# A decode block with its gradients: the middle regrouped, and second-pass transposes as products with the identity

## The chip, the cores and the metric

The kernel runs on one core of a Trainium2 chip. The metric is the device time of one execution in microseconds (us). TensorE is called PE here, VectorE DVE, ScalarE ACT, GpSimd POOL and SyncE SP, as in the profile; PEld is PE's loading of weights.

## The reference

One transformer block for a single token per sequence, forward and backward: a layer norm, attention against a cache of 4096 keys and values (batch 2, 32 heads, head size 128), a residual, a second layer norm and an MLP with relu (640 to 1728 to 640). Results are the output and the gradients of seven inputs.

```python
def _fwd_reference(A_x, A_k_cache, A_v_cache, A_wq, A_wo, B_x, B_w1, B_w2):
    ...
        q = (lambda x, *d: x.transpose(*d))((x @ wq).reshape(B, Sq, Hq, Dh), 0, 2, 1, 3)
        scores = jnp.einsum("bhqd,bhkd->bhqk", q, k) * (Dh ** -0.5)
        p = _softmax(scores, axis=-1)
        o = jnp.einsum("bhqk,bhkd->bhqd", p, v)
        return (lambda x, *d: x.transpose(*d))(o, 0, 2, 1, 3).reshape(B, Sq, Hq * Dh) @ wo
    ...
        h = jnp.einsum("bsd,df->bsf", x, w1)
        h = jnp.maximum(h, zero)
        return jnp.einsum("bsf,fd->bsd", h, w2)
    x = A_x
    h = x + _A_ref(_layernorm(x, axis=-1), A_k_cache, A_v_cache, A_wq, A_wo)
    h2 = h + _B_ref(_layernorm(h, axis=-1), B_w1, B_w2)
    return h2

def reference(A_x, A_k_cache, A_v_cache, A_wq, A_wo, B_w1, B_w2, B_x, grad_out):
    ...
    _out, _vjp = jax.vjp(_f, A_x, A_k_cache, A_v_cache, A_wq, A_wo, B_w1, B_w2)
    _grads = _vjp(grad_out)
```

Everything is bf16. The two caches are 64 tiles of 1 MB each (one per batch and head); their gradients, as large, are outer products of a column of length 4096 and a row of length 128.

## The kernel before

A pair is one batch and one head; there are 64. The **first pass** (`p1_iter`, one iteration per pair in a software pipeline three deep) loads a K and a V tile. It transposes K in four groups of eight 128x128 blocks on PE (`transpose_group`, line 264; ACT evicts a group from PSUM at line 269, or DVE at line 267 for the last group of the first iterations), multiplies by q (line 275), takes the softmax, and forms with V the attention output and a 128x128 matrix MT that the backward pass needs (lines 294 and 310, scaled by ACT at line 396). The **second pass** (`p2_iter`, one iteration per pair, index j) loads V again as W, transposes it in the same way, multiplies it by the gradient of the attention output, and forms the gradients gV and gK as outer products on DVE (line 533, two halves each), which POOL's queue stores (lines 577 and 593).

Between the passes stands the **middle** of each batch (`middle_gen`): the product with wo, layer norm, w1, relu, w2, the output row, then backward: the products of grad_out with w2 (`ga`), of the masked result with w1 (`gx2`), the backward layer norm, and products with wo in four groups of eight heads, each of which ends with the mark `("go", b, g)`. Those backward products are done on DVE by `ttr` (line 426), a multiplication with a row that is spread over the partitions (`bcast_cols`), summed along the row. After both middles `fin_gen` forms the weight gradients: `rows_of` (line 611) turns columns to rows, `outer_rows` forms output tiles of up to 512 columns with PE (line 635), evicts them by ACT or DVE (lines 638 and 640) and stores them (line 643); at last five columns of wq are loaded again (line 667), transposed and multiplied (line 676).

The order of all instructions is written out by hand: the generators are run against each other, each engine takes its instructions in that order, and SP issues the loads in the order of a list (`queue`), as tiles come free. The middles and `fin_gen` are background generators in a list `bg`, taken one after the other. After each step of a pass, `bg_step` adds a rate to a credit and runs background steps until the credit is used; a step costs 0.35, or what it yields (0.9 for a `ttr`). A first-pass iteration has 8 such steps, a second-pass one 5. `bg_until` runs the background at once where a pair needs a mark that isn't there. `plan` starts the second pass at first-pass iteration `P2_AT`, in every second iteration, until the first pass ends; from there it runs alone.

PSUM has two buffers for transposes (tag `tps`), three for scores and one each for `m`, `tiny` and `mid`; the background shares `mid`. SBUF has seven tiles of 1 MB for loads and three for gV and gK.

Of the kernel before, what the change touches and what calls it, by code (L numbers as in the profile page):

```python
# [9 lines left out]
ALU = mybir.AluOpType  # L10
# [5 lines left out]
def kernel(  # L16
# [97 lines left out]
    OU = cols.tile([128, B, H, 2], FP32)  # L114
    P_bf = cols.tile([128, B * H, NSC], BF16)
    nc.vector.memset(acol[:], 0.0)
    nc.vector.memset(ghfc[:], 0.0)
# [14 lines left out]
    def ln_fwd(xs, nb, xh, rstd):  # L132

        def st(name, dt=FP32):
            return small.tile([128, nb], dt, tag=f"ln_{name}{nb}", bufs=1, name=f"ln_{name}")
        ssum = st("ssum")
        nc.vector.reduce_sum(out=ssum[:], in_=xs, axis=AX.X)
        t1 = colsum(ssum[:], nb)
        yield
        mean = st("mean")  # L140
        nc.vector.tensor_scalar(out=mean[:], in0=t1[:, 0:nb], scalar1=1.0 / D, scalar2=None, op0=ALU.mult)
        cent = small.tile([128, nb, ND], FP32, tag=f"ln_cent{nb}", bufs=1, name="ln_cent")
        nc.vector.tensor_tensor(out=cent[:], in0=xs, in1=bc(mean[:], ND), op=ALU.subtract)
# [3 lines left out]
        nc.vector.reduce_sum(out=vs[:], in_=sq[:], axis=AX.X)  # L147
        t2 = colsum(vs[:], nb)
# [23 lines left out]
        yield  # L172

    def ln_bwd(gh, xh, rstd, add, dst, nb):

        def t3(name):
# [5 lines left out]
        nc.vector.reduce_sum(out=mm[:, 0, :], in_=gh, axis=AX.X)  # L182
        nc.vector.reduce_sum(out=mm[:, 1, :], in_=prod[:], axis=AX.X)
        t = colsum(mm[:].rearrange("p a b -> p (a b)"), 2 * nb)
        yield
# [8 lines left out]
        nc.vector.tensor_tensor(out=dst.rearrange("p c b -> p b c"), in0=u1[:],  # L194
                                in1=add.rearrange("p c b -> p b c"), op=ALU.add)
        yield

# [62 lines left out]

    def transpose_group(nat, g, dve=False):
        t_ps = pst([128, GT, 128], BF16, "tps", "t_ps")
        for j in range(GT):
            nc.tensor.transpose(t_ps[:, j, :], nat[:, g * GT + j, :], ident_bf[:])  # L264
        t_sb = mats.tile([128, GT, 128], BF16, tag="XT", bufs=5, name="t_sb")
        if dve:
            nc.vector.tensor_copy(out=t_sb[:], in_=t_ps[:])  # L267
        else:
            nc.scalar.copy(out=t_sb[:], in_=t_ps[:])  # L269
        return t_sb  # L270
# [161 lines left out]
    def middle_gen(b):  # L432
# [3 lines left out]
        for c in range(ND):  # L436
            for h in range(H):
                nc.tensor.matmul(a_ps[:, c:c + 1], lhsT=wo_t[:, h, c * 128:(c + 1) * 128], rhs=OFc[:, h, b:b + 1],
                                 start=(h == 0), stop=(h == H - 1))
                if h % 16 == 15:  # L440
                    yield
# [8 lines left out]
        for cf in range(NF):  # L450
            kc = f_kc(cf)
            for c in range(ND):
                nc.tensor.matmul(hf_ps[0:kc, cf:cf + 1], lhsT=w1_t[:, c, cf * 128:cf * 128 + kc],
                                 rhs=x2c[:, c, b:b + 1], start=(c == 0), stop=(c == ND - 1))
            if cf % 4 == 3:
                yield
        nc.vector.tensor_scalar(out=acol[:, 0:NFF, b], in0=hf_ps[:, 0:NFF], scalar1=0.0, scalar2=None, op0=ALU.max)
        if F_rem:
            nc.vector.tensor_scalar(out=acol[0:F_rem, NFF, b:b + 1], in0=hf_ps[0:F_rem, NFF:NF],
                                    scalar1=0.0, scalar2=None, op0=ALU.max)  # L460
        yield
        m_ps = pst([128, ND], FP32, "mid", "mlp_ps")
        for c in range(ND):
            for cf in range(NF):
                kc = f_kc(cf)
                nc.tensor.matmul(m_ps[:, c:c + 1], lhsT=w2_t[0:kc, cf, c * 128:(c + 1) * 128],
                                 rhs=acol[0:kc, cf, b:b + 1], start=(cf == 0), stop=(cf == NF - 1))
            if c % 2 == 1:
                yield
        ml_bf = small.tile([128, ND], BF16, tag="ml_bf", bufs=1, name="ml_bf")  # L470
        nc.vector.tensor_copy(out=ml_bf[:], in_=m_ps[:])
        y_bf = small.tile([128, ND], BF16, tag="y_bf", bufs=1, name="y_bf")
        nc.vector.tensor_tensor(out=y_bf[:], in0=h1c[:, :, b], in1=ml_bf[:], op=ALU.add)
        yield
        store_row(y_bf[:], ND, out_0[b].rearrange("s (c p) -> (s c) p", p=128))
        yield
# [11 lines left out]
        nc.vector.tensor_tensor(out=ghfc[:, :, b], in0=ga[:], in1=mask[:], op=ALU.mult)  # L488
        yield
# [14 lines left out]
        for g in range(H // GH):  # L504
# [7 lines left out]
            nc.vector.tensor_tensor(out=pr[:], in0=goc[:, hs, b], in1=OU[:, b, hs, 0], op=ALU.mult)  # L512
            yield
            d_ps = pst([128, 2, GH], FP32, "mid", "d_ps")
            nc.tensor.matmul(d_ps[:, 0, :], lhsT=ones_f32[:], rhs=pr[:], start=True, stop=True)
# [8 lines left out]
            nc.vector.tensor_scalar(out=GQc[:, hs, b], in0=ud[:], scalar1=SCALE, scalar2=None, op0=ALU.mult)  # L524
            yield ("go", b, g)


# [23 lines left out]

    def p2_iter(j):

        c = S2[j] if j < NP1 else None
        p = S2[j - 1] if j - 1 in S2 else None
        if c is not None:
            b, h = pairs[j]
            go = goc[:, h, b:b + 1]
            if "rb" not in c:
                p2_rows(j)  # L560
            c["T0"] = transpose_group(c["W"], 0)
            gV = take("g", [128, NSC, 128], "gV")
# [9 lines left out]
        if c is not None:  # L572
            c["dp"] = pst([128, NSC], FP32, "sps", "dp_ps")
            c["T1"] = transpose_group(c["W"], 1)
            matvec_group(c["dp"], c.pop("T0"), 0, go)
# [4 lines left out]
        if c is not None:  # L580
            c["T2"] = transpose_group(c["W"], 2)
            matvec_group(c["dp"], c.pop("T1"), 1, go)
# [4 lines left out]
        if c is not None:  # L587
            c["T3"] = transpose_group(c["W"], 3)
            give(c["Wg"])
# [29 lines left out]
    def outer_rows(pool, L, nrow, R, N, out_ap, cc):  # L619
# [4 lines left out]
        for c0 in range(0, cc, grp):  # L624
# [4 lines left out]
            for k in range(gn):  # L629
                n0 = 0  # L630
                while n0 < N:
# [9 lines left out]
                    n0 += nn  # L641
                    yield
            nc.gpsimd.dma_start(out=out_v[:, c0:c0 + gn, :], in_=ot[0:P, 0:gn, :])
# [71 lines left out]

    M0_ITERS = 17
    P2_AT = H + 2 + M0_ITERS
    plan = []
    i = j = 0
# [10 lines left out]
    for n, (ii, jj) in enumerate(plan):  # L730
# [34 lines left out]
    for n, (i, j) in enumerate(plan):  # L765
# [64 lines left out]
```

## Time and profile before

| | |
|---|---|
| Median of 3 runs | 1136.31 us (1134.83 to 1139.74) |
| Profiled execution | 1132.04 us |
| Its span, first to last instruction | 1130.1 us |
| Busy: PE, DVE, ACT, POOL | 75%, 64%, 56%, 9% |
| Read and written | 221.48 MB and 149.13 MB |
| Mean granted PE clock | 0.723 |

Times are those of one profiled execution. A row of the groups gives line, engine, operation and tiles, then the count, the busy time, the mean duration in ns, and the idle time before it with what ended it. The granted clock is the share of full speed that the chip gave PE. A DMA share is the mean busy share of the core's 16 DMA engines.

### The profile page before, as it was taken

To read this page: it belongs to the slowest core of one execution; us is meant where nothing else is said; L and a number is where in the kernel's file an instruction comes from. 1 tells how busy PE (TensorE), PEld (TensorE's weight loads), DVE (VectorE), ACT (ScalarE), POOL (GpSimd) and SP (SyncE) were. 2 spreads that over 40 slices of the span, in tenths; PEclk is the share of its full clock that TensorE was granted. 3 is DMA by queue.
4 is the path that set the end of the run, shared out by engine and by line. 5 is a ranking of instruction groups with operands and counts; after the bars stand their busy time and mean duration, and the time that the engine had idled before them with its cause. 6 is when DMAs were issued, how large, how long until landed. Compare 5 with 4: busy or idle time off the path is not lost.

```text
span 1130.1 us, 32280 instructions
## 1 busy us (share of the span) xinstructions
PE 845.2 (75%) x14111; PEld 724.3 (64%) x14111; DVE 717.7 (64%) x1693; ACT 634.0 (56%) x945; POOL 100.6 (9%) x218
## 2 busy tenths in 40 slices
PE   6999999989889878878673545478887875565572
PEld 5988889988878778778563534354564444454562
DVE  3666666655778778556668789945455452345676
ACT  4565555655756667665373644366666643354562
POOL 0000000000000001001111111111111110001121
PEclk9999998986979898888575766555555555575555
DMA  9999999975777598999999989858897687479987
GB/s 360 370 405 406 408 403 400 392 266 188 273 251 239 218 351 336 351 371 378 364 395 371 385 342 348 327 224 321 312 333 298 268 340 267 178 276 416 388 346 325
DMA packets 59757, 372.70 MB, mean 330 GB/s; under 512 B 5760, under 2 KB 15424, under 8 KB 17376
## 3 DMA queue, kind: packets, MB, share of 16 engines
q1 hardware_dynamic: 38960, 221.50, 52.4%
q0 software_dynamic: 20656, 149.14, 32.5%
q8 instruction: 110, 1.80, 0.6%
q14 instruction: 31, 0.25, 0.1%
HBM read 221.48 MB, written 149.13 MB: 328 GB/s over the span
## 4 chain that ended last, share of the span: by engine, by line
PE 43%; DMA 18%; DVE 17%; issue 10%; ACT 10%; POOL 1%; SPq 0%; ACTq 0%; POOLq 0%; DVEq 0%
PE t_ps L264 17%; PE m_ps L294 9%; DMA out_dram<-gV 9%; DVE gK L533 5%; ACT t_sb L269 5%; DMA Wt<-in_A_v_cache_dram 4%; PE m_ps L310 4%; PE o_ps L635 3%; PE s_ps L275 3%; DVE pk L300 3%; DVE junk L426 3%; DVE gV L533 3%; DMA wqs<-in_A_wq_dram 2%; ACT ot L638 1%; PE rw_ps L611 1%
## 5 line engine op out<-in xcount | busy, mean ns | idle before, releaser
L269 ACT COPY t_sb<-t_ps 128x1024 bf16<-128x1024 bf16 x489 | 488.8, 1015 | 234.4 <-PE t_ps L264 228.4
L264 PE MATMUL t_ps<-ident_bf,Wt 128*128 128x128 bf16 x2048 | 234.0, 285 | 12.6 <-DMA Wt<-in_A_v_cache_dram 12.2
L275 PEld LDWEIGHTS <-t_sb 128*128 128x128 bf16 x4096 | 168.9, 103 | 95.8 <-ACT t_sb L269 89.8
L264 PEld LDWEIGHTS <-Wt 128*128 128x128 bf16 x2048 | 182.0, 130 | 58.6 <-issue 45.3
L300 DVE TENSOR_TENSOR pk<-Kt,ep 128x1024 bf16<-128x1024 bf16 x256 | 174.6, 684 | 39.7 <-ACT ep L343 39.6
L294 PE MATMUL m_ps<-pk,Vt 128*128 128x129 bf16 x2048 | 190.7, 233 | 0.9 <-issue 0.9
L533 DVE TENSOR_TENSOR gV<-rb,pp 128x2048 bf16<-128x2048 bf16 x128 | 156.0, 1218 | 51.7 <-POOL pp L549 18.0
L264 PE MATMUL t_ps<-ident_bf,Kt 128*128 128x128 bf16 x2048 | 173.2, 233 | 7.0 <-DMA Kt<-in_A_k_cache_dram 5.0
L533 DVE TENSOR_TENSOR gK<-rb,gsp 128x2048 bf16<-128x2048 bf16 x128 | 153.2, 1218 | 32.7 <-DMA out_dram<-gV 32.5
L275 PE MATMUL dp_ps<-goc,t_sb 128*128 128x1 bf16 x2048 | 96.9, 168 | 69.0 <-ACT t_sb L269 65.9
L294 PEld LDWEIGHTS <-Vt 128*128 128x128 bf16 x2048 | 134.5, 103 | 6.0 <-issue 1.3
L264 PEld LDWEIGHTS <-Kt 128*128 128x128 bf16 x2048 | 131.8, 104 | 8.9 <-DMA Kt<-in_A_k_cache_dram 5.6
L267 DVE COPY t_sb<-t_ps 128x1024 bf16<-128x1024 bf16 x43 | 29.7, 692 | 110.8 <-PE t_ps L264 105.4
L577 POOL DMA_DIRECT2D out_dram<-gV x64 | 34.2, 535 | 729.4 <-DVE gV L533 694.7
L275 PE MATMUL s_ps<-qc,t_sb 128*128 128x1 bf16 x2048 | 89.4, 164 | 1.4 <-DVE gsp L568 0.4
L396 ACT ACTIVATE MT<-m_ps,rtot 128x128 bf16<-128x128 f32 x64 | 23.5, 368 | 106.3 <-PE m_ps L294 106.3
L640 DVE CAST ot<-o_ps 128x128 bf16<-128x128 f32 (+2 forms) x80 | 33.6, 420 | 71.9 <-PE o_ps L635 70.4
L310 PEld LDWEIGHTS <-Kt 128*128 128x128 bf16 x2048 | 64.5, 97 | 18.7 <-issue 17.4
L310 PE MATMUL m_ps<-ep,Kt 128*128 128x1 bf16 x2048 | 70.9, 164 | 7.0 <-ACT OU L397 6.5
L547 ACT CAST rb<-rb_ps 128x256 bf16<-128x256 f32 x64 | 24.0, 376 | 81.2 <-DVE gK L533 63.9
L638 ACT CAST ot<-o_ps 128x512 bf16<-128x512 f32 (+1 forms) x80 | 47.0, 587 | 22.6 <-PE o_ps L635 20.8
L593 POOL DMA_DIRECT2D out_dram<-gK x64 | 34.1, 532 | 223.5 <-DVE gK L533 210.2
(168 smaller groups left out, 738.0 us busy)
## 6 DMA issues: line engine op xcount, KB each, us to landing
Kt<-in_A_k_cache_dram SPq DMA_DIRECT2D x64, 1024.0 KB, 8.5
Vt<-in_A_v_cache_dram SPq DMA_DIRECT2D x64, 1024.0 KB, 8.4
Wt<-in_A_v_cache_dram SPq DMA_DIRECT2D x64, 1024.0 KB, 8.8
out_dram<-gV POOLq DMA_DIRECT2D x64, 1024.0 KB, 6.4
out_dram<-gK POOLq DMA_DIRECT2D x64, 1024.0 KB, 7.7
wo_t<-in_A_wo_dram SPq DMA_DIRECT2D x4, 1280.0 KB, 11.7
out_dram<-ot POOLq DMA_DIRECT2D x5, 1024.0 KB, 8.9
wqs<-in_A_wq_dram SPq DMA_DIRECT2D x5, 1024.0 KB, 8.1
```

The costliest lines, as they stand in the source:

```text
L264: nc.tensor.transpose(t_ps[:, j, :], nat[:, g * GT + j, :], ident_bf[:])
L269: nc.scalar.copy(out=t_sb[:], in_=t_ps[:])
L275: nc.tensor.matmul(dst[:, sc:sc + 1], lhsT=t_sb[:, j, :], rhs=vec, start=True, stop=True)
L294: nc.tensor.matmul(r["m"][:, 0:129], lhsT=r["V"][:, sc, :], rhs=r["pk"][sc // GT][:, sc % GT, 0:129], start=False, stop=(sc == NSC - 1))
L300: nc.vector.tensor_tensor(out=pk[:, :, 0:128].rearrange("p s (a two) -> p s a two", two=2), in0=p["K"][:, sl, :].rearrange("p s (a two) -> ...
L310: nc.tensor.matmul(r["m"][:, 129:130], lhsT=r["K"][:, sc, :], rhs=r["ep"][:, sc, 0:1], start=(sc == 0), stop=False)
L426: nc.vector.tensor_tensor_reduce(out=junk[0:kc, 0:width], in0=in0, in1=in1, scale=1.0, scalar=0.0, op0=ALU.mult, op1=ALU.add, accum_out=acc)
L533: nc.vector.tensor_tensor(out=pairs_view(dst[:, sl, :]), in0=row.rearrange("p (a two) -> p a two", two=2)[:, None, :, :].to_broadcast([128 ...
L577: nc.gpsimd.dma_start(out=natural(out_3, b, h), in_=gV[:])
L593: nc.gpsimd.dma_start(out=natural(out_2, bp, hp), in_=gK[:])
L635: nc.tensor.matmul(o_ps[0:P, 0:nn], lhsT=L[:, bass.ds(c0 + k, P, step=cc)], rhs=R[:, n0:n0 + nn], start=True, stop=True)
L638: nc.scalar.copy(out=ot[0:P, k, n0:n0 + nn], in_=o_ps[0:P, 0:nn])
```

## The change

- The products of grad_out with w2, which don't depend on the forward pass, leave the middle: a generator `ga_gen` computes them for both batches, as a background of the first pass from iteration 14 on. w2 is loaded first of the weights, then w1, then wo.
- In the middle, the forward product with w2 and the output row come last, behind the four groups of wo. Several places get a second yield between a DVE result and the PE instruction that uses it, and the wo and w1 products yield twice as often.
- `M0_ITERS` goes from 17 to 11, so the second pass starts six first-pass iterations earlier. The rates are new, and a tile of `outer_rows` costs 0.5 of credit, not 0.35. `fin_gen` starts when the second middle has ended.
- Where no first pass runs beside it, the second pass transposes V by plain products with the identity, whose result is float32 in PSUM: four blocks to a PSUM buffer instead of eight, and two evictions for a group.

```diff
+    ga = cols.tile([128, B, NF], FP32)
+    nc.vector.memset(ga[:], 0.0)
...
         nc.vector.reduce_sum(out=ssum[:], in_=xs, axis=AX.X)
+        yield
+        yield
         t1 = colsum(ssum[:], nb)
...
-    def transpose_group(nat, g, dve=False):
-        t_ps = pst([128, GT, 128], BF16, "tps", "t_ps")
-        for j in range(GT):
-            nc.tensor.transpose(t_ps[:, j, :], nat[:, g * GT + j, :], ident_bf[:])
+    def transpose_group(nat, g, dve=False, plain=False):
+
         t_sb = mats.tile([128, GT, 128], BF16, tag="XT", bufs=5, name="t_sb")
-        if dve:
-            nc.vector.tensor_copy(out=t_sb[:], in_=t_ps[:])
-        else:
-            nc.scalar.copy(out=t_sb[:], in_=t_ps[:])
+        n = GT // 2 if plain else GT
+        for k in range(0, GT, n):
+            t_ps = pst([128, n, 128], FP32 if plain else BF16, "tps", "t_ps")
+            for j in range(n):
+                if plain:
+                    nc.tensor.matmul(t_ps[:, j, :], lhsT=nat[:, g * GT + k + j, :], rhs=ident_bf[:],
+                                     start=True, stop=True)
+                else:
+                    nc.tensor.transpose(t_ps[:, j, :], nat[:, g * GT + k + j, :], ident_bf[:])
+            if dve:
+                nc.vector.tensor_copy(out=t_sb[:, k:k + n, :], in_=t_ps[:])
+            else:
+                nc.scalar.copy(out=t_sb[:, k:k + n, :], in_=t_ps[:])
...
-                if h % 16 == 15:
+                if h % 8 == 7:
                     yield
...
-            if cf % 4 == 3:
+            if cf % 2 == 1:
                 yield
...
-        yield
-        m_ps = pst([128, ND], FP32, "mid", "mlp_ps")
...
-        store_row(y_bf[:], ND, out_0[b].rearrange("s (c p) -> (s c) p", p=128))
-        yield
-        gbc = cols.tile([128, D], BF16, tag="rowbc", name="gbc")
-        yield from bcast_cols(one(gc, b), ND, lambda c: 128, gbc)
-        ga = small.tile([128, NF], FP32, tag="ga", bufs=1, name="ga")
-        if F_rem:
-            nc.gpsimd.memset(ga[:], 0.0)
-        for c in range(NF):
-            kc = f_kc(c)
-            ttr(w2_t[0:kc, c, :], gbc[0:kc, :], ga[0:kc, c:c + 1], D, kc)
-            yield 0.9
...
-        nc.vector.tensor_tensor(out=ghfc[:, :, b], in0=ga[:], in1=mask[:], op=ALU.mult)
+        nc.vector.tensor_tensor(out=ghfc[:, :, b], in0=ga[:, b, :], in1=mask[:], op=ALU.mult)
...
             yield ("go", b, g)
+        m_ps = pst([128, ND], FP32, "mid", "mlp_ps")
...
+        store_row(y_bf[:], ND, out_0[b].rearrange("s (c p) -> (s c) p", p=128))
+        yield ("y", b)
+
+    def ga_gen():
+
+        for b in range(B):
+            gbc = cols.tile([128, D], BF16, tag="rowbc", name="gbc")
+            yield from bcast_cols(one(gc, b), ND, lambda c: 128, gbc)
+            for c in range(NF):
+                kc = f_kc(c)
+                ttr(w2_t[0:kc, c, :], gbc[0:kc, :], ga[0:kc, b, c:c + 1], D, kc)
+                yield 0.9
...
-                    yield
+                    yield 0.5
...
-    M0_ITERS = 17
+    M0_ITERS = 11
     P2_AT = H + 2 + M0_ITERS
+    RATES = (0.2, 0.5, 0.12, 0.42, 0.88)
...
-            queue.append(("w", (ii - 8) // 3))
+            queue.append(("w", (5, 4, 0, 1, 2, 3)[(ii - 8) // 3]))
...
-            gens.append(p2_iter(j))
+            gens.append(p2_iter(j, i is None))
...
-        if "m0" in done and i is None and ("gh1", 1) in done and fin is None:
+        if i is None and ("y", 1) in done and fin is None:
...
+        if i == 14:
+            bg.append(("ga", ga_gen()))
-        rate = 0.42 if i is not None and i < P2_AT else 0.16 if i is not None else 0.48 if fin is None else 1.0
+        rate = RATES[0 if i is not None and i <= H + 1 else 1 if j is None else 2 if i is not None else
+                     3 if j <= H else 4]
```

More of the change, by code (lines that the diff above doesn't have):

```diff
@@ L147, in ln_fwd @@
         nc.vector.reduce_sum(out=vs[:], in_=sq[:], axis=AX.X)
+        yield
+        yield
         t2 = colsum(vs[:], nb)
@@ L172, in ln_fwd @@
         yield
+        yield
     def ln_bwd(gh, xh, rstd, add, dst, nb):
@@ L183, in ln_bwd @@
         nc.vector.reduce_sum(out=mm[:, 1, :], in_=prod[:], axis=AX.X)
+        yield
+        yield
         t = colsum(mm[:].rearrange("p a b -> p (a b)"), 2 * nb)
@@ L195, in ln_bwd @@
                                 in1=add.rearrange("p c b -> p b c"), op=ALU.add)
+        yield
         yield
@@ L460, in middle_gen @@
                                     scalar1=0.0, scalar2=None, op0=ALU.max)
-        yield
-        m_ps = pst([128, ND], FP32, "mid", "mlp_ps")
[L463 to L468, printed above, removed]
-                yield
[L470 to L473, printed above, removed]
-        yield
-        store_row(y_bf[:], ND, out_0[b].rearrange("s (c p) -> (s c) p", p=128))
-        yield
-        gbc = cols.tile([128, D], BF16, tag="rowbc", name="gbc")
-        yield from bcast_cols(one(gc, b), ND, lambda c: 128, gbc)
-        ga = small.tile([128, NF], FP32, tag="ga", bufs=1, name="ga")
-        if F_rem:
-            nc.gpsimd.memset(ga[:], 0.0)
-        for c in range(NF):
-            kc = f_kc(c)
-            ttr(w2_t[0:kc, c, :], gbc[0:kc, :], ga[0:kc, c:c + 1], D, kc)
-            yield 0.9
         mask = small.tile([128, NF], FP32, tag="mask", bufs=1, name="mask")
         nc.vector.tensor_single_scalar(out=mask[:], in_=acol[:, :, b], scalar=0.0, op=ALU.is_gt)
-        nc.vector.tensor_tensor(out=ghfc[:, :, b], in0=ga[:], in1=mask[:], op=ALU.mult)
+        nc.vector.tensor_tensor(out=ghfc[:, :, b], in0=ga[:, b, :], in1=mask[:], op=ALU.mult)
+        yield
         yield
@@ L513, in middle_gen @@
             yield
+            yield
             d_ps = pst([128, 2, GH], FP32, "mid", "d_ps")
@@ L525, in middle_gen @@
             yield ("go", b, g)
+        m_ps = pst([128, ND], FP32, "mid", "mlp_ps")
+        for c in range(ND):
+            for cf in range(NF):
+                kc = f_kc(cf)
+                nc.tensor.matmul(m_ps[:, c:c + 1], lhsT=w2_t[0:kc, cf, c * 128:(c + 1) * 128],
+                                 rhs=acol[0:kc, cf, b:b + 1], start=(cf == 0), stop=(cf == NF - 1))
+            yield
+        ml_bf = small.tile([128, ND], BF16, tag="ml_bf", bufs=1, name="ml_bf")
+        nc.vector.tensor_copy(out=ml_bf[:], in_=m_ps[:])
+        y_bf = small.tile([128, ND], BF16, tag="y_bf", bufs=1, name="y_bf")
+        nc.vector.tensor_tensor(out=y_bf[:], in0=h1c[:, :, b], in1=ml_bf[:], op=ALU.add)
+        yield
+        yield
+        store_row(y_bf[:], ND, out_0[b].rearrange("s (c p) -> (s c) p", p=128))
[8 more added lines that the diff above has]
+                yield 0.9
     def pairs_view(t):
@@ L550, in p2_rows, with p2_iter @@
         S2.setdefault(j, {}).update(rb=rb, pp=pp)
-    def p2_iter(j):
+    def p2_iter(j, plain):
         c = S2[j] if j < NP1 else None
@@ L560, in p2_iter @@
                 p2_rows(j)
-            c["T0"] = transpose_group(c["W"], 0)
+            c["T0"] = transpose_group(c["W"], 0, plain=plain)
             gV = take("g", [128, NSC, 128], "gV")
@@ L573, in p2_iter @@
             c["dp"] = pst([128, NSC], FP32, "sps", "dp_ps")
-            c["T1"] = transpose_group(c["W"], 1)
+            c["T1"] = transpose_group(c["W"], 1, plain=plain)
             matvec_group(c["dp"], c.pop("T0"), 0, go)
@@ L580, in p2_iter @@
         if c is not None:
-            c["T2"] = transpose_group(c["W"], 2)
+            c["T2"] = transpose_group(c["W"], 2, plain=plain)
             matvec_group(c["dp"], c.pop("T1"), 1, go)
@@ L587, in p2_iter @@
         if c is not None:
-            c["T3"] = transpose_group(c["W"], 3)
+            c["T3"] = transpose_group(c["W"], 3, plain=plain)
             give(c["Wg"])
@@ L641, in outer_rows @@
                     n0 += nn
-                    yield
+                    yield 0.5
             nc.gpsimd.dma_start(out=out_v[:, c0:c0 + gn, :], in_=ot[0:P, 0:gn, :])
```

## The prediction

> **What bounds the kernel now.** I read the page first (span, slices), then the busy times by stage, then the iterations in each stage, then the groups and waits that price the edits. In the page's slices each digit is tenths.
>
> ```profile
> span 1130.1 us, 32280 instructions
> ...
> PEclk9999998986979898888575766555555555575555
> DMA  9999999975777598999999989858897687479987
> ```
>
> DMA is saturated for most of the span, with three holes: slices 9 to 14, slice 27 and slices 31 to 36. So I cut the span into six stages: first pass alone (A), first pass with the first batch's middle (B), both passes (C), second pass with the second middle (D), second pass with the final products (E), second pass alone (F). The columns are window, length, busy us of PE, PEld, DVE, ACT and POOL, granted clock, DMA share, GB/s.
>
> ```profile
> 0.00:233.00 233.00, 214.25 (x4494) 196.76 (x4495) 142.42 (x493) 133.52 (x235) 2.06 (x9) 0.98 1.00 392
> 233.00:384.00 151.00, 134.00 (x2621) 122.32 (x2618) 105.57 (x372) 91.95 (x152) 0.00 (x0) 0.82 0.66 231
> 384.00:531.00 147.00, 120.50 (x2375) 111.45 (x2376) 101.34 (x260) 98.05 (x150) 11.83 (x23) 0.87 0.90 348
> 531.00:735.00 204.00, 110.10 (x1822) 97.26 (x1819) 161.21 (x294) 98.16 (x122) 32.84 (x67) 0.63 0.93 363
> 735.00:1000.00 265.00, 194.70 (x1771) 134.00 (x1771) 125.95 (x195) 145.94 (x211) 31.81 (x69) 0.51 0.73 275
> 1000.00:1130.00 130.00, 71.69 (x1042) 62.52 (x1039) 81.22 (x84) 66.39 (x79) 22.00 (x50) 0.58 0.92 371
> ...
> DMA packets 59757, 372.70 MB, mean 330 GB/s; under 512 B 5760, under 2 KB 15424, under 8 KB 17376
> ...
> out_dram<-gV POOLq DMA_DIRECT2D x64, 1024.0 KB, 6.4
> ```
>
> At stage A's 392 GB/s all 372.70 MB would take 951 us; 179 us are lost, and by stage (length less bytes over 392) 62 of them in B, 79 in E, and 7 to 17 in each of C, D and F. A second-pass iteration moves three such tiles of 1024 KB (a V, a gV, a gK), 3.1 MB. The change moves no byte of traffic away, so what it can win lies in B and E.
>
> The next rows give the pace. The first four count one ACT scaling of m_ps per first-pass iteration, the others one gV store issue per second-pass iteration.
>
> ```profile
> 90.00:215.00 125.00, 6.98 (x19) 0.96 1.02 401
> 233.00:271.00 38.00, 0.98 (x3) 0.66 0.53 185
> 271.00:384.00 113.00, 5.52 (x15) 0.87 0.71 246
> 384.00:531.00 147.00, 5.51 (x15) 0.87 0.90 348
> ...
> 531.00:668.00 137.00, 8.36 (x16) 0.63 0.96 379
> 668.00:735.00 67.00, 3.35 (x7) 0.63 0.87 330
> 735.00:1000.00 265.00, 9.58 (x18) 0.51 0.73 275
> 1046.00:1119.00 73.00, 5.85 (x11) 0.53 0.90 364
> ```
>
> A first-pass iteration takes 125/19 = 6.58 us in A, 113/15 = 7.53 us in B's later part, and 147/15 = 9.8 us in C. A second-pass iteration takes 137/16 = 8.56 and 67/7 = 9.57 us in D, and 73/11 = 6.64 us with nothing beside it.
>
> **What the change moves, in steps.** The background generator is paced by credits, which can be counted from the code: a first-pass iteration gives 8 slots, a second-pass one 5, each worth the rate. The w2 products (two batches of 2×0.35 + 14×0.9 = 13.3) run at 8×0.2 = 1.6 an iteration, so over iterations 14 to 30. A middle is now 66.75 credits (69.55 before): the first one gives its first group of output gradients at iteration 43 and ends in 53; the second starts with the second pass alone, at 5×0.42 = 2.1 an iteration to j=32 and 4.4 after, and ends at j=37 (30 before). The final products cost 107.65 credits (82.6 before, because each tile now costs 0.5), 4.4 an iteration: j=38 to 62 (31 to 46 before). The second pass begins beside first-pass iteration 45, not 51, so 11 of its iterations, not 8, lie beside the first.
>
> Rows for the prices:
>
> ```profile
> L269 ACT COPY t_sb<-t_ps 128x1024 bf16<-128x1024 bf16 x489 | 488.8, 1015 | 234.4 <-PE t_ps L264 228.4
> L264 PE MATMUL t_ps<-ident_bf,Wt 128*128 128x128 bf16 x2048 | 234.0, 285 | 12.6 <-DMA Wt<-in_A_v_cache_dram 12.2 <-ACT t_sb L269 0.3
> L638 ACT CAST ot<-o_ps 128x512 bf16<-128x512 f32 x62 | 36.5, 589 | 17.4 <-PE o_ps L635 15.7 <-PE t_ps L264 1.0
> L426 DVE CUSTOM_DVE_ANT_0 junk<-w_t,gbc 128x640 bf16<-128x640 bf16 x26 | 21.3, 817 | 1.4 <-ACT gbc L413 1.4
> L611 PE MATMUL rw_ps<-ident_bf,OFc 128*2 128x128 bf16 x32 | 4.7, 300 | 4.1 <-ACT OFr L613 4.1
> ...
> 258.89 0.99 PE mlp_ps L466 x28
> ...
> PE csum L126 <- DVE lb_mm L183: 15.6, 3, 13.7
> PE d_ps L515 <- DVE pr L512: 31.2, 5, 8.1
> PE bc_ps L410 <- DVE ghfc L488: 12.0, 1, 12.0
> PE t_ps L264 <- DMA wqs<-in_A_wq_dram: 16.8, 3, 6.9
> ```
>
> *Stage A, w2 products added.* 28 × 0.817 = 22.9 us of DVE over 17 iterations, 1.35 each. DVE is busy 142.42 of 233 us, so it rises to about 0.8 in those iterations, under DMA at 1.00; free if DMA covers all of it. What is not covered is a product standing in front of the maximum that PE needs next: nothing at best, 0.6 us an iteration (half of the 1.35, rounded down) at worst. I take 0.3: +5 us (0 to 10), so A ends at 238. If the DMA cover goes, 22.9 us is the whole price. The new load order (w2, w1, then wo) changes no byte; wo is last needed at iteration 34 and queued at 24.
>
> *Stage B, 11 iterations instead of 17.* The first 3.6 of them carry the wo and w1 products and the layer norm: three such iterations took 38 us against 3×6.58, so 18 us over. The 70 products with w2 for the output now come behind the gradients (70/28 × 0.99 = 2.5 us on B's chain), and the doubled yields put a slot between a DVE result and the PE instruction that needs it. The three PE waits of the last fence, 58.8 us over both batches and all stages, are what those yields address; which of them the time really paid for I can't see. I keep 12 of the 18 us (6 to 18). Then 7.4 iterations at 7.53 us, raised for the rate 0.5 against 0.42: the 0.95 us over A's 6.58 becomes 1.13, so 7.7 us each. 3.6×6.58 + 12 + 7.4×7.7 = 93 us (85 to 102), where B took 151.
>
> *Stage C.* 21 iterations at the 9.8 us of before: 206 us (196 to 215). It is bound by DMA at 348 GB/s with three more second-pass iterations of 3.1 MB in it; the lower rate (0.12 against 0.16) frees engines that aren't the bound. The output row of batch 0 and its store go past SP's queue here rather than in B; SP's later V and K loads wait behind it for the row copy, which two yields separate: 0 to 2 us, taken as 0. So the second pass alone starts at 238 + 93 + 206 = 537 with 53 iterations left, where it started at 531 with 56.
>
> *Stage D, 27 iterations.* 22 at 8.56 us (DMA at 0.96, so a rate of 0.42 against 0.48 buys nothing) and 5 at 9.57: 236 us (225 to 245), where DMA alone needs 27 × 3.1 MB at 392 GB/s = 216.
>
> *Stages E and F, 26 iterations.* Over the bare 6.64 us, E's 18 iterations cost 265 − 18×6.64 = 145 us: 160 output tiles, 32 row copies and the five wq columns, whose loads PE waits for in program order. That work is the same; it is spread over 25 iterations. 26×6.64 + 145 = 318 us (285 to 330). DMA alone would need less: E and F moved 275×0.265 + 371×0.130 = 121 MB, and 8 iterations fewer leave 96 MB, 245 us at 392 GB/s. The lower end hides a quarter of the 145 under it.
>
> *Products in place of transposes.* Operands, columns and weight loads are the same, so PE does not change: four products with the identity (rw_ps) take 300 ns apiece at half clock beside the transposes' 285. [...] PSUM now holds float32, so a group needs two evictions of 512 columns: 2×0.589 = 1.18 us against 1.015, 0.65 us of ACT an iteration. ACT is busy 98.16 of 204 us in D and 145.94 of 265 in E, so it is covered by DMA in D and by PE or DMA in E, not where PE waits for ACT. I charge half of it in E's 25 iterations, +8 us; without cover 53×0.65 = 34, at best 0.
>
> Does the product raise the clock? The next rows are L264's transposes in windows of 3.41 us, cut where the recorded clock steps; the columns are window, length, PE busy and count of those transposes, granted clock, DMA share, GB/s:
>
> ```profile
> 569.32:572.74 3.42, 2.82 (x24) 0.50 0.99 321
> 572.74:576.15 3.41, 2.02 (x27) 1.00 0.90 312
> 671.72:675.14 3.42, 2.27 (x32) 1.00 0.90 211
> 675.14:678.55 3.41, 1.87 (x25) 1.00 1.01 413
> 951.62:955.03 3.41, 2.77 (x24) 0.50 0.74 219
> 955.03:958.45 3.42, 2.03 (x16) 0.50 0.96 395
> ```
>
> 24 transposes at 0.50 are followed by a window at 1.00, and 25 to 32 of them hold it there; 16 to 24 elsewhere leave it at 0.50. So transposes do lift the clock, from some 24 in a window. An iteration has 32 of them, and at 8.56 us a window of 3.41 us holds 13. Making them products changes neither number: 0 us. [...]
>
> *Sum.* 238 + 93 + 206 + 236 + 318 + 8, and 12 from the last gV store (1118) to the end: 1111 us of span, against 1130.1. The profiled execution took 1132.04 us, 2 over its span, and the median of the runs is 4 over that: 1111 + 2 + 4 = **1117 us**, 1.7% below 1136.31.
>
> **The rivals.**
>
> 1. *The clock rises.* If products count and transposes do not, PE's 194.70 busy us of E, all at half clock, shrink towards half, and D and E fall to their DMA time: 216 + 245 in place of 236 + 326, so 101 less: 1016 us. For it: E's clock is 0.51 with PE busy 0.73 of the time. Against it: the six windows above. Chance 0.06.
>
> 2. *The half-size groups stall PE (slower).* Two PSUM tiles held two groups ahead, and now hold one. Place: the second half of a group waits for ACT to have evicted the same half of the group before, behind whatever cast ACT has queued; the matvecs, the row broadcasts and the final tiles are queued behind it on PE, and the gK products on DVE wait for those. Price: up to the eviction's 0.59 us in each of four groups, 2.4 us an iteration over 53 iterations where nothing covers it; with half of that 1.2×53 = 64, less the 8 charged: 1173 us. It decides from (1142 + 8 − 1117)/53 = 0.62 us an iteration. For it: ACT is the busiest neighbour of PE in E, and PE already waits for its casts. Against it: in D, DMA at 0.96 leaves 2 us of slack an iteration. Chance 0.16.
>
> 3. *The final products run over.* They are counted out at j=62 of 63, and each wait for a free buffer takes 0.35 of credit without work; before, the count says 46 and the last came at about 48. Two more iterations late, and two wq columns with their loads of 8 us stand alone at the end: 25 us, so 1142, no change. Chance 0.2.
>
> **How the numbers follow.** Forecast 0.58, its own range 1090 to 1134. A measurement of this kernel can tell about 0.5%: 1130.6 to 1142. Faster: most of the forecast (0.55), the first rival (0.06) and the near end of the third (0.05): 0.66. Same: 0.03 of the forecast, 0.10 of the third, 0.02 of the second: 0.15. Slower: the rest, 0.19. The range takes 1078 (the lower ends of B, C and E are not all to be had at once) to 1150, which leaves out the first rival and most of the second.
>
> **What would show it.** In the changed profile: the first pass still at 6.3 to 6.9 us an iteration between iterations 14 and 30 (A right); the first gV store near 335 us (B right; before 355 even with the stalls kept); the first gV store of the second pass alone near 540 us; the clock still 0.5 to 0.6 from there on (otherwise rival 1); waits of t_ps for t_sb on ACT under 20 us in all (otherwise rival 2); the last wq column before the last gV store (otherwise rival 3). The forecast is wrong if stage C runs slower than 10.3 us an iteration, since it then hands back what B won.

## The result, and the profile after

The changed kernel takes 1096.93 us (median of 4 runs, 1090.07 to 1098.32), the kernel before 1138.03 (median of 4, 1134.83 to 1143.64): a ratio of 0.9622, 95% interval 0.9564 to 0.9679. The forecast was 1117 us and 1.7% faster: the sign was right, and the gain of 41 us is a little more than twice the 19 us that were forecast. The profiled execution took 1098.32 us, with a span of 1096.6.

From the page of the changed kernel, the slices in tenths:

```profile
span 1096.6 us, 32501 instructions
...
PEclk9999888995689978888775555855655555555556
DMA  9999999895565888999899999999679999999835
```

Counted from 1, the hole at slices 10 to 13 is still there. In place of the second one, slices 31 to 36 of before, there are a shallow one at slices 29 and 30 and a short one at 39 and 40. The clock stays near 0.5 over most of the second half (0.57, 0.51 and 0.50 in the rows from 561 to 1076 us below). Busy times by stage of the changed kernel, cut where its own stages end (window, length, busy us of PE, PEld, DVE, ACT, POOL, granted clock, DMA share, GB/s):

```profile
0.00:246.00 246.00, 220.54 (x4505) 203.23 (x4505) 162.84 (x550) 134.62 (x239) 1.87 (x8) 0.95 0.97 372
246.00:351.00 105.00, 94.41 (x1750) 87.47 (x1748) 67.83 (x243) 62.01 (x103) 0.00 (x0) 0.74 0.61 217
351.00:561.00 210.00, 176.46 (x3414) 163.05 (x3412) 142.39 (x372) 139.34 (x212) 14.23 (x31) 0.85 0.88 340
561.00:796.00 235.00, 144.99 (x2136) 133.13 (x2136) 174.31 (x290) 126.92 (x251) 36.36 (x82) 0.57 0.93 369
796.00:1002.00 206.00, 182.73 (x1622) 125.04 (x1620) 130.49 (x182) 155.55 (x297) 35.18 (x78) 0.51 0.95 374
1002.00:1076.00 74.00, 45.63 (x589) 39.35 (x587) 29.95 (x49) 29.59 (x48) 6.22 (x14) 0.50 0.62 241
1076.00:1096.00 20.00, 7.30 (x107) 6.23 (x107) 9.88 (x12) 6.72 (x13) 2.42 (x6) 0.67 0.64 263
```

Where did the time go? The twelfth gV store (j=11) is a point that both kernels pass. First the kernel before, then the changed one, in the timeline of POOL (start, us, engine, line):

```profile
565.05 0.53 POOL L577 DMA_DIRECT2D out_dram<-gV  x1 [4.35 <-DVE gV L533]
```

```profile
564.59 0.53 POOL L596 DMA_DIRECT2D out_dram<-gV  x1 [2.97 <-DVE gV L552]
```

They pass it at the same time. Such a point moves by some us from one execution to the next: in the five other kept traces that have the changed kernel's first half it comes at 558 to 570 us, in the two others that have the first half of before at 566 and 571. So what was done to the first half, the w2 products, the six iterations taken out of stage B, the earlier second pass, has won a few us at most by then: A is 13 us longer, B 46 shorter, C 63 longer, and the three D iterations that are saved (531 to 565) took 34. In these two executions the whole gain comes after j=11, and most of it where the final products run. The gV issues there, first before, then after (the count is of issues, then granted clock, DMA share, GB/s):

```profile
751.00:921.00 170.00, 6.39 (x12) 0.51 0.80 305
```

```profile
796.00:1002.00 206.00, 10.63 (x20) 0.51 0.95 374
1002.00:1076.00 74.00, 2.60 (x5) 0.50 0.62 241
```

With tiles beside it a second-pass iteration took 170/12 = 14.2 us before and 206/20 = 10.3 after, at the same clock. DMA went from 0.80 to 0.95.

### The profile page after: what moved, and what is told of

It is laid out like the page before. It is cut to its first block, busy times and chain, and to the rows that moved or that the text cites. A ratio compares the mean times of both kernels' runs of the same rounds, so it can differ in the third digit from the quotient of the medians.

```text
span 1096.6 us, 32501 instructions
## 1 busy us (share of the span) xinstructions
PE 872.1 (80%) x14111; PEld 757.5 (69%) x14111; DVE 717.7 (65%) x1694; ACT 654.7 (60%) x1157; POOL 96.3 (9%) x216
## 4 chain that ended last, share of the span: by engine, by line
PE 42%; DMA 21%; DVE 20%; issue 9%; ACT 7%; POOL 1%; SPq 0%; POOLq 0%; DVEq 0%; ACTq 0%
PE t_ps L282 12%; DMA out_dram<-gV 10%; PE m_ps L311 9%; DMA Wt<-in_A_v_cache_dram 6%; DVE gK L552 5%; PE t_ps L279 5%; DVE pk L317 5%; ACT t_sb L286 4%; PE o_ps L654 4%; PE m_ps L327 4%; DVE junk L443 4%; PE s_ps L292 3%; DVE gV L552 2%; DMA out_dram<-ot 2%; PE dp_ps L292 1%
## 5 line engine op out<-in xcount | busy, mean ns | idle before, releaser
L286 ACT COPY t_sb<-t_ps 128x1024 bf16<-128x1024 bf16 x277 | 277.4, 1013 | 116.7 <-PE t_ps L282 113.6
L286 ACT CAST t_sb<-t_ps 128x512 bf16<-128x512 f32 x424 | 228.4, 590 | 97.2 <-PE t_ps L279 92.7
L279 PE MATMUL t_ps<-ident_bf,Wt 128*128 128x128 bf16 x1696 | 216.6, 297 | 36.2 <-ACT t_sb L286 29.8
L279 PEld LDWEIGHTS <-Wt 128*128 128x128 bf16 x1696 | 165.7, 134 | 89.8 <-issue 79.1
L311 PE MATMUL m_ps<-pk,Vt 128*128 128x129 bf16 x2048 | 197.8, 238 | 0.5 <-issue 0.4
L292 PEld LDWEIGHTS <-t_sb 128*128 128x128 bf16 x4096 | 179.2, 105 | 10.9 <-issue 5.5
L282 PE MATMUL t_ps<-ident_bf,Kt 128*128 128x128 bf16 x2048 | 178.1, 238 | 9.3 <-DMA Kt<-in_A_k_cache_dram 8.1
L282 PEld LDWEIGHTS <-Kt 128*128 128x128 bf16 x2048 | 136.3, 106 | 11.1 <-DMA Kt<-in_A_k_cache_dram 9.4
L311 PEld LDWEIGHTS <-Vt 128*128 128x128 bf16 x2048 | 139.0, 105 | 5.8 <-issue 0.9
L292 PE MATMUL dp_ps<-goc,t_sb 128*128 128x1 bf16 x2048 | 99.2, 169 | 0.8 <-ACT t_sb L286 0.5
L327 PEld LDWEIGHTS <-Kt 128*128 128x128 bf16 x2048 | 64.5, 97 | 18.3 <-issue 16.8
```

What stands on the lines that cost most here:

```text
L279: nc.tensor.matmul(t_ps[:, j, :], lhsT=nat[:, g * GT + k + j, :], rhs=ident_bf[:], start=True, stop=True)
L282: nc.tensor.transpose(t_ps[:, j, :], nat[:, g * GT + k + j, :], ident_bf[:])
L286: nc.scalar.copy(out=t_sb[:, k:k + n, :], in_=t_ps[:])
L292: nc.tensor.matmul(dst[:, sc:sc + 1], lhsT=t_sb[:, j, :], rhs=vec, start=True, stop=True)
L311: nc.tensor.matmul(r["m"][:, 0:129], lhsT=r["V"][:, sc, :], rhs=r["pk"][sc // GT][:, sc % GT, 0:129], start=False, stop=(sc == NSC - 1))
L327: nc.tensor.matmul(r["m"][:, 129:130], lhsT=r["K"][:, sc, :], rhs=r["ep"][:, sc, 0:1], start=(sc == 0), stop=False)
```

## The experiments

The theories at the start: the *pacing* of the final products makes the gain; or the *products with the identity* do, by the clock or by shorter evictions; or the *early start* with the regrouped middle does. Ratios are to the kernel before, timed beside each, with 95% intervals.

**Undo the products alone.**

```diff
-            gens.append(p2_iter(j, i is None))
+            gens.append(p2_iter(j, False))
```

> The changed kernel with the second pass's V transposed as before, by transposes with bf16 results and one eviction a group; all else as changed. Pacing theory (the gain of the late stages comes from spreading the final products until DMA covers them, and the products with the identity are worth nothing): within 0.5% of the changed kernel, 1092 to 1102 us, ratio to the kernel before about 0.962, granted clock from 561 us on 0.50 to 0.57 as in the changed kernel. Product theory (the products raise the clock, or their half-size evictions shorten PE's path): slower than the changed kernel by 15 us or more, ratio 0.975 or above. Stall theory (half-size groups cost PE time): faster by 8 us or more, ratio below 0.955.

1102.37 us, 0.9691 (0.9635 to 0.9747): at the edge of what the pacing theory allowed, and short of the 0.975 of the product theory. The interval overlaps the changed kernel's, and the profiled executions differ by 0.7 us in span, so a gain by the products can't be told here, and a small one can't be excluded. Stages of this kernel, from its D on:

```profile
561.00:796.00 235.00, 136.94 (x2142) 120.98 (x2142) 172.61 (x287) 117.82 (x142) 36.22 (x80) 0.58 0.92 366
796.00:1010.00 214.00, 185.18 (x1634) 127.24 (x1634) 132.37 (x183) 146.53 (x215) 35.23 (x79) 0.50 0.94 367
1010.00:1076.00 66.00, 41.99 (x571) 37.02 (x571) 27.77 (x46) 27.14 (x31) 5.22 (x12) 0.53 0.63 248
```

The clock is 0.50 to 0.58 with transposes and 0.50 to 0.57 with products. ACT is busy 9 us less in each of the first two windows, and the time doesn't fall.

**Do the products alone**, in the kernel before: the changed `transpose_group`, with `plain=i is None`.

> The kernel before with the products with the identity where no first pass runs beside the second, all else as before. Pacing theory: within 0.7% of the kernel before, 1130 to 1145 us. Product theory: faster by 15 us or more, ratio 0.987 or below. Stall theory: slower by 8 us or more, since PE and ACT bound stage E (735 to 1000 us), which DMA does not cover here.

1135.13 us, 0.9977 (0.9944 to 1.001): no change that can be told, and none where DMA gives no cover. Its stage E:

```profile
735.00:1000.00 265.00, 198.28 (x1784) 135.96 (x1781) 127.44 (x196) 155.72 (x285) 31.73 (x69) 0.50 0.72 275
```

The row of before had ACT at 145.94 in the same 265 us. So 9.8 us more of ACT cost nothing that can be told: neither the product theory nor the stall theory holds. Nor did the clock rise: over all ten runs its mean is 0.698, against 0.713 in the 13 runs of the kernel before beside them.

**Undo the pacing alone.**

```diff
-                    yield 0.5
+                    yield
...
-    RATES = (0.2, 0.5, 0.12, 0.42, 0.88)
+    RATES = (0.2, 0.5, 0.12, 0.42, 1.0)
```

> The changed kernel with the old pacing of the final products: a tile costs 0.35 of credit again and the last rate is 1.0, so by the count they end at iteration 54 and not at 62. Pacing theory: the stretch of tiles is no longer under DMA, 15 to 30 us slower than the changed kernel, ratio 0.975 to 0.99, and the tile stretch moves under 320 GB/s. Rival (the gain comes from the earlier start of the second pass and the split waits): within 0.7% of the changed kernel.

1117.82 us, 0.9819 (0.9765 to 0.9873): half of the gain is gone, as the pacing theory said. **Do the pacing alone**, in the kernel before:

```diff
-                    yield
+                    yield 0.5
...
-        rate = ... else 0.48 if fin is None else 1.0
+        rate = ... else 0.48 if fin is None else 0.88
```

> The kernel before with the new pacing of the final products alone: a tile costs 0.5, and the rate with them is 0.88, so by the count they end near iteration 55 and not 46. Pacing theory: 15 to 30 us faster than the kernel before, ratio 0.973 to 0.987. Rival (early start and split waits): within 0.7% of the kernel before.

1098.82 us, 0.9637 (0.9589 to 0.9685): two numbers give the gain of the whole change, more than the 15 to 30 us that were expected of them. The gV issues in the stretch of tiles, with the old pace in the changed kernel and then with the new pace in the kernel before (each profile is the longest of its kernel's four runs, 1127.96 and 1104.15 us):

```profile
807.00:979.00 172.00, 6.91 (x13) 0.50 0.82 315
```

```profile
749.00:952.00 203.00, 10.65 (x20) 0.50 0.91 356
```

172/13 = 13.2 us at the old pace and 203/20 = 10.2 at the new, each near what the other kernel takes at that pace (14.2 and 10.3). With 0.88/0.5 a slot brings 1.8 tiles instead of 2.9, 8.8 an iteration instead of 14.3; the same 160 tiles then stand beside more of the iterations that move 3.1 MB each.

**Undo the early start alone**, `M0_ITERS` 17 in the changed kernel.

> The changed kernel with the second pass started at first-pass iteration 51 again and not 45, all else as changed. If the earlier start is worth its three iterations (the prediction's reading of stage B): 20 to 30 us slower than the changed kernel, ratio to the kernel before 0.98 to 0.99. If stage C hands back what B wins: within 0.7% of the changed kernel, ratio 0.955 to 0.97.

1107.27 us, 0.9716 (0.9667 to 0.9764): some 10 us slower, between the two expectations. **Do the early start alone**, `M0_ITERS` 11 in the kernel before, with the first middle's rate at 0.55 so that it is ready:

> The kernel before with the early start of the second pass alone (iteration 45, first middle's rate 0.55); the final products at the old pace. The changed kernel at the old pace was 1.8% faster than the kernel before. If the early start made that: ratio 0.975 to 0.988. If it came from the later and shorter second half (the second middle slowed, the final products begun at iteration 38): within 0.7% of the kernel before.

1134.39 us, 0.9999 (0.9967 to 1.0032): nothing. Its j=11 store is issued at 561 us, the kernel before's at 565, and its last one at 1122 us, behind the 1118 of before. **Early start and pacing together**, without the rest:

> The kernel before with two parts alone: the new pacing of the final products (0.5 a tile, rate 0.88) and the early start of the second pass at iteration 45, for which the first middle's rate is 0.55; the w2 products stay in the middle, the waits unsplit, V transposed by transposes. If the regrouped middle (w2 products in the first pass, split waits, output row last) is what lets the early start pay: 8 us or more slower than the changed kernel, ratio 0.97 or above. If the regrouping only moves its cost into stage A: within 0.7% of the changed kernel, ratio 0.955 to 0.97.

1096.59 us, 0.9627 (0.9574 to 0.968), the changed kernel's time. So with the pacing in place the regrouped middle, the w2 products in the first pass, the early start and the products with the identity add up to nothing that can be told. The late start with the regrouped middle is the slowest combination at the new pace; perhaps the regrouping has a cost that its early start pays back, but its interval (0.9667 to 0.9764) overlaps at its edge both the changed kernel's and that of the pacing alone, so this is not shown. What remains open is why the changed kernel at the old pace is still 1.8% faster, when its early start alone is worth nothing in the kernel before: the later begin of the final products, the split waits, another part of the regrouping, or several together; no run takes these apart.

**Leave the w2 products out.**

```diff
-                ttr(w2_t[0:kc, c, :], gbc[0:kc, :], ga[0:kc, b, c:c + 1], D, kc)
                 yield 0.9
```

> The changed kernel with the 28 DVE products of grad_out with w2 left out of the first pass (their broadcasts and credits stay, so the pacing is the same; the gradients that pass the MLP are then zero, and every later instruction still runs). If the products on DVE are what makes stage A 13 us longer: the ACT scaling of iteration 34's m_ps comes near 245 us, not 257, and the run ends 8 to 14 us before the changed kernel, 1083 to 1089 us. If the new order of the weight loads is the cause: stage A as in the changed kernel, and 1092 to 1100 us.

1091.18 us, 0.9562 (0.9503 to 0.9622). The median is 6 us below the changed kernel's, less than the 8 to 14 expected of the products, and the intervals overlap, so the traces are the better measure. The scaling of iteration 34's m_ps comes at 249 us instead of 257 (243 in the kernel before); in the six other traces that are the same up to there it comes at 254 to 258, so the products cost some 5 to 10 us. The rows are the stretch from 96 to 202 us, of the changed kernel, with two of PE's waits in it (us in total, times, longest), and then of this one:

```profile
96.00:202.00 106.00, 96.46 (x1936) 89.38 (x1934) 76.14 (x248) 56.80 (x106) 0.00 (x0) 0.89 0.98 378
...
PE mx_ps L344 <- DVE rmax L401: 4.6, 6, 0.8
PE nb_ps L356 <- DVE gmax L346: 1.5, 4, 0.4
```

```profile
96.00:202.00 106.00, 98.00 (x2122) 90.16 (x2120) 67.85 (x228) 61.26 (x113) 0.00 (x0) 0.97 1.02 400
```

DVE is busy 0.72 of the time with the products, far from full, yet PE gets through 1936 matmuls instead of 2122, and the clock falls from 0.97 to 0.89. The products stand ahead of the maximum that PE waits for: 6.1 us by the two rows, where this kernel and the one before have at most 0.2 of such waits in the same stretch. Of the 13 us of stage A some 8 are the products; the rest is not settled, and the new load order was not tried by itself.

**The wq columns, loaded one ahead** (`load_col(c + 1)` before column c is transposed):

> The changed kernel with each wq column of the last product loaded one column ahead, so that PE does not stand before a load of 8.5 us five times. If those loads set the length of the stretch from 1002 to 1076 us (74 us for 5 iterations of 6.6 us): 20 to 30 us faster than the changed kernel, 1067 to 1077 us, and PE's waits for wqs under 8 us. If the stores of gV and gK or the DVE set it: within 0.7% of the changed kernel.

1096.72 us, 0.9636 (0.9585 to 0.9686): no change. In this stretch PE waits for a wq load only once, 8.6 us here and 8.8 in the changed kernel, and not five times as the expectation had it. The same stretch in this kernel:

```profile
999.00:1072.00 73.00, 45.18 (x587) 39.00 (x584) 29.28 (x47) 29.48 (x47) 5.64 (x14) 0.50 0.63 243
```

**The wq columns first of the final products:**

> The changed kernel with the wq columns loaded one ahead and multiplied first of the final products, where V loads still fill the DMA queues, and the output tiles after them to the end. If the wq stretch is long because little else is left to move beside it: 25 to 40 us faster than the changed kernel, 1057 to 1072 us, with DMA over 0.9 up to the last 20 us. If PE's waits for the columns only move to another place: within 0.7% of the changed kernel.

1092.92 us, 0.96 (0.9555 to 0.9644): not told from the changed kernel either, and far from the 25 to 40 us. So the loads are not the cause. The chain of waits of the changed kernel in that stretch shows what is:

```profile
1014.13 1.05 PE t_ps L282 x8
1015.26 1.02 ACT t_sb L286
1016.70 0.89 PE t_ps L282 x8
1017.68 0.70 DVE t_sb L284
```

PE transposes a group, waits for its eviction, multiplies it, and only then transposes the next. **One group ahead:**

```diff
                 t_sb = transpose_group(st, g, g % 2 == 1)
                 ...
                 yield
-                for j in range(GT):
-                    ...
-                yield
+                if pend:
+                    gx_part(*pend.pop())
+                    yield
+                pend.append((c, g, t_sb))
+        gx_part(*pend.pop())
```

> The changed kernel with the wq columns loaded one ahead and, new, each group of them transposed before the group ahead of it is multiplied, so that PE does not stand before the eviction it has just caused. If the chain transpose, eviction, product, transpose sets the 74 us from 1002 to 1076 us: that stretch shrinks to 45 to 60 us and the run to 1068 to 1085 us, ratio 0.94 to 0.955. If the second pass's own iterations set it: within 0.7% of the changed kernel.

1079.22 us, 0.9464 (0.9406 to 0.9522), with the stretch 56 us long instead of 74:

```profile
1002.00:1058.00 56.00, 37.60 (x571) 34.02 (x568) 28.16 (x47) 28.33 (x45) 5.59 (x13) 0.62 0.74 293
```

The clock went from 0.50 to 0.62 in it, and PE's busy time from 45.6 us to 37.6, so a part of the 18 us may be the clock and not the shorter chain; no run takes the two apart.

The same on the kernel with the pacing and the early start alone:

> The kernel of the early start and the new pacing alone, with the wq columns loaded ahead and multiplied one group late. In it 6 second-pass iterations follow the final products. If the chain through the evictions sets the wq stretch: 10 to 25 us faster than the same kernel without that. If DMA, which still has V tiles to load there, sets it: within 0.7% of it.

1076.6 us, 0.9475 (0.9418 to 0.9532). It is 20 us faster than the same kernel without that. Both beat the changed kernel; the two can't be told apart.

## Why the prediction was wrong

By its own steps, from the stage rows above:

- **A, 238 us; measured 246.** The price of the w2 products (+5, 0 to 10) was too low: +13, of which some 8 are the products. The reason given, a product ahead of what PE needs, held; DVE's busy share was the wrong cover to look at. An iteration took 123/16 = 7.7 us there (first row below), not the 6.3 to 6.9 that were the mark.
- **B, 93; measured 105.** The step that said the moved output row and the doubled yields would take a third off the wo and w1 stretch failed. The five iterations with those products take 54 us (second row, and PE's waits in them below it), where the first five of stage B took 53 before (last row): nothing came off.

```profile
110.00:233.00 123.00, 5.88 (x16) 0.90 0.96 367
...
246.00:300.00 54.00, 50.42 (x897) 47.13 (x895) 23.93 (x93) 29.10 (x47) 0.00 (x0) 0.59 0.55 193
PE hf_ps L470 <- DVE x2c L177: 1.8, 1, 1.8
PE a_ps L455 <- DVE OFc L450: 1.2, 1, 1.2
...
233.00:286.00 53.00, 47.52 (x958) 44.20 (x955) 28.59 (x107) 28.13 (x45) 0.00 (x0) 0.71 0.59 209
```

PE hardly waits in them. It is busy 50.4 of the 54 us, at a clock of 0.59. The 58.8 us of waits that the prediction named were counted over the whole execution. In the kernel before, 54.7 of them lie between 531 and 735 us, in stage D (first three rows); there they still are, in part, in the changed kernel (561 to 796 us, last four):

```profile
PE d_ps L515 <- DVE pr L512: 29.0, 4, 8.1
PE csum L126 <- DVE lb_mm L183: 13.7, 1, 13.7
PE bc_ps L410 <- DVE ghfc L488: 12.0, 1, 12.0
...
PE d_ps L509 <- DVE pr L505: 29.8, 4, 9.5
PE t_ps L279 <- ACT t_sb L286: 26.9, 11, 6.1
PE csum L128 <- DVE ln_ssum L139: 14.5, 1, 14.5
PE csum L128 <- DVE lb_mm L190: 8.1, 1, 8.1
```

The first gV store came at 355 us, where 335 was the mark for B right and 355 for stalls that stay.
- **C, 206; measured 210**, and **D, 236; measured 235**: right. So the start of the second pass alone, put at 537, came at 561. The 24 us that A to C should have won by j=11 were more than the whole forecast gain of 19, and they were nearly 0; the early start alone is worth nothing (0.9999).
- **E and F, 318 + 8 + 12 = 338; measured 300** (206 + 74 + 20). This is the step that decided. "That work is the same; it is spread over 25 iterations", at 145 us over the bare 6.64 us. The two rows split that price: 186 − 14×6.64 = 93 us for tiles and rows, 79 − 4×6.64 = 52 for the wq columns.

```profile
735.00:921.00 186.00, 7.45 (x14) 0.51 0.78 295
921.00:1000.00 79.00, 2.13 (x4) 0.50 0.61 228
```

By the same reckoning the changed kernel spent 206 − 20×6.64 = 73 us and 74 − 5×6.64 = 41: 114, not 145. The price of a tile was taken from a stretch in which tiles were so dense that PE stood before their evictions, 14.2 us an iteration with DMA at 0.80. The next rows are those waits, between 751 and 921 us before and between 796 and 1002 after: 18.7 us in 12 iterations, then 9.1 in 20.

```profile
PE o_ps L635 <- ACT ot L638: 15.6, 30, 0.8
PE o_ps L635 <- DVE ot L640: 3.1, 9, 0.4
...
PE o_ps L654 <- DVE ot L659: 5.0, 5, 2.3
PE o_ps L654 <- ACT ot L657: 4.1, 6, 1.9
```

At the lower density DMA is at 0.95, so part of the tiles' work seems to lie under transfers that an iteration waits for anyway. On the wq columns PE waited 16.8 us for loads before and 8.8 after. The working had the DMA time, 245 us, as a floor, but its lower end of 285 hid only a quarter of the 145. The pacing runs show that this term is enough for the whole gain: 0.9637 with the new pace alone. Without it half of the gain is left (0.9819), by the way that stays open above.
- **Products, 0 us on the clock and +8 on ACT.** The clock is as said, 0.51 in the stretch of tiles before and after. The 8 us were not there: ACT's extra time cost nothing even in the uncovered stage E of the kernel before (0.9977).
- **Offset.** The runs' median was put 4 us above the profiled execution, as before; it came 1 us below. That is 6 of the 20 us between 1117 and 1096.93. The steps above make the other 14: +8, +12, +4, −1 and −38 are −15, and the last 0.6 us of the span lie behind the last window.

So the sign was right by luck. The forecast gain was to come from the earlier start, which won next to nothing; the measured one came from the price of the final products, which the prediction held the same. The errors of +24 us up to C and −38 in E and F partly cancel.

The rivals: the clock did not rise (0.57, 0.51 and 0.50 in the three stages from 561 us on, 0.63, 0.51 and 0.58 in the last three of before). The half-size groups do make PE wait, 29.8 us over the whole execution in t_ps for t_sb, 26.9 of it in the rows above, where 20 was the mark for that rival. But with transposes PE waits 36.2 us for the same evictions, only one step later, in dp_ps for t_sb (`x1_transposes`):

```profile
PE dp_ps L292 <- ACT t_sb L286: 36.2, 19, 8.3
```

So these waits moved and did not grow. The final products did not run over: the wq stretch ended at 1076 us, ahead of the last gV store at 1085.

## What to carry to other kernels

In the kernel before, background work that was dense for a while and then gone cost twice: PE stood before its evictions (18.7 us in 12 iterations) with DMA at 0.80, and later the iterations ran with DMA at 0.90 and nothing beside it. Spread it until the transfers of the loop it stands in cover it, DMA at 0.95 here; two pacing numbers gave the whole gain, and one group transposed ahead of its product, in a short stretch with DMA at 0.62, won another 1.6%. Take the price of such work at the density that it will have, not at the one it had. And before an edit is credited with a wait, look in which stage that wait lies: 54.7 of the 58.8 us here lay in another stage than the one they were to shorten.

## What was not expected of the hardware

Counted in the traces of the changed kernel and of the kernel before, products with the identity and transposes can't be told apart by the clock that follows them. There the granted clock is at 0.50 or at 1.00, and its 44 and 46 steps lie whole multiples of 3.41 us apart. For each window of that length I added up the columns of the matmuls that start in it and fill all 128 rows, and took the clock of the next window. In the changed kernel, windows in which products with the identity make 0.7 or more of the columns are followed by the full clock 0 times of 87 below 2850 columns, 4 of 6 up to 3000, 4 of 5 up to 3150 and 3 of 4 above. Windows of the kernel before with as large a share of transposes: 3 of 112 below 2850, 3 of 11, 6 of 9, and 32 of 32 above 3150. From 2850 on that is 11 of 15 with products and 41 of 52 with transposes. Two neighbours each from the changed kernel (PE busy and number of identity products, those on an edge included; granted clock, DMA share, GB/s). By the count of columns, other wide products included, the first window holds 3217 columns, the last two 2712 and 2834:

```profile
687.42:690.83 3.41, 2.86 (x24) 0.50 0.76 317
690.84:694.25 3.41, 2.31 (x26) 1.00 1.05 324
...
724.97:728.38 3.41, 2.69 (x22) 0.50 1.02 425
728.38:731.79 3.41, 2.90 (x24) 0.50 1.08 389
```

The stretch of output tiles gives other numbers. Between 796 and 1002 us of the changed kernel PE is busy 182.73 of 206 us at a clock of 0.51; 24 of the 60 windows hold more than 3000 columns, up to 3536, if the tiles' matmuls, which fill two rows, are added in, and none of the 24 is followed by the full clock; without them no window there holds more than 2953. No run tried these matmuls by themselves.

The slow start of stage B, between 250 and 295 us of the changed kernel, has the clock at 0.51 with PE busy 42.65 of the 45 us and 2520 columns a window on average. Of its 721 matmuls 214 are products with wo and w1 of one column each, 9.0 us of that busy time.
